# One chunk's half of a Strassen pass's second product is moved between the products of the pass before it

## The chip, the cores and the metric

The kernel runs on one core of a Trainium2 chip. The metric is the device time of one execution in microseconds (us), as a median of several runs. Times inside an execution come from the hardware profiler and are counted from the first instruction.

## The reference

A depthwise causal convolution with 7 softmax-normalised taps for each of 8 heads, then a block that normalises each row, multiplies by two matrices with a ReLU between them, and adds the result to the row:

```
# x: (8, 4224, 192) f32, weight: (8, 7)
w = softmax(weight, axis=-1)                      # per head
y[b,s,h,:] = sum_k w[h,k] * x_pad[b, s+k, h, :]   # 24 channels per head
xn = (y - mean(y)) / sqrt(var(y) + 1e-6) * g_ln   # over the 192 channels
out = y + max(xn @ w_ch1, 0) @ w_ch2              # 192 -> 768 -> 192
```

Everything is 32-bit floating point.

## The kernel before

**Groups.** The 33,792 rows are cut into 18 groups of at most 16 rows for each of 128 partitions. The first three are short and use plain matrix products. The other 15 (numbers 3 to 17, 2048 rows each, the last one with a few exceptions) take the first product (192 to 768, "up", `up_mixed`) and the second (768 to 192, "down", `down_fast`) each by seven half-size products instead of eight: a Strassen-Winograd scheme, in which sums of blocks are formed before and after. While TensorE does group g, VectorE convolves the rows of group g+1, ScalarE scales the outputs of group g-1, and GpSimd starts the DMAs.

**The up stage of a group.** `up_mixed` makes two passes over the 768 hidden features, in chunks of 128: the *small pass* (`one`) does one chunk of each half of the features, the *large pass* (`two`) two chunks of each half. Each pass has the same seven products, always in this order: a11·b11, a12·b21, s2·t0, s3·t1, s1·b12, a22·t2, s4·b22 (in the text "products 1 to 7"; aij are quarters of the group's rows, s1 to s4 sums of these, bij and t0 to t2 quarters of the weights and their sums). `rows_of_tiles` (L523) issues a product: for each of three blocks c of 32 channels, and each chunk i, four matmuls, one for each block q of 32 rows of the TensorE array, which work beside each other. So a product of the small pass has 12 matmuls of 32x128 weights by 256 columns, and one of the large pass 24. The profile counts two records for each matmul.

**The banks.** PSUM has eight banks of 512 f32 for each partition. The up stage splits them into two sets of four, X and Y (L689). Block q writes bank q of the set; chunk i writes columns 256·i to 256·i+255 of it. In the small pass there is one chunk only, so the upper 256 columns of each bank lie unused. The products alternate: in the small pass X, Y, X, Y, X, Y, X; in the large pass Y, X, Y, X, Y, X, Y. One of the two sets is the pass's *chain*: X in the small pass, Y in the large one. Products 1, 3, 5 and 7 add onto each other in it, and each is copied out in between. Product 2 stands alone in the other set, and products 4 and 6 add onto each other there.

**Copying out.** After each product, the set is copied to SBUF by ScalarE (`evict`, L646, the instruction at L660), before the next product that writes this set can start. In the small pass that is 1024 elements for each partition, in two halves of 512 (banks 0 and 1, banks 2 and 3); in the large pass 2048 elements at once. `close` (L662) handles products 2, 5 and 6, which belong onto a sum that is already in SBUF: it copies into a scratch tile and then adds this to the finished product by an accumulating DMA that GpSimd starts (`add_by_dma`, L615), or lets VectorE add directly from PSUM (L666). In the large pass, product 2 is closed chunk by chunk: two copies of 1024 elements to the tile `parts_cs`, and two such DMAs onto `c11` (L724). ScalarE then applies ReLU to `c11` in place (L673), much later, after the copy of product 5.

**Order.** All engines run their instructions in the order written; the schedule is made by hand, and semaphores are placed where one instruction needs what another wrote or frees. The order in the large pass (L709 to L759): product 1 into Y; copy Y to `c11`; product 2 into X; two copies from X to `parts_cs` with the DMAs; a scaling (L938); product 3 into Y; copy Y to `c21`; ReLU; product 4 into X; copy X to `c22`; product 5 into Y; `close`; product 6 into X; VectorE adds X (L666); product 7 into Y; copy with ReLU. The down stage (L859) begins with a bank that product 6 used.

Of the kernel before, what the change touches and what calls it, by code (L numbers as in the profile page):

```python
# [16 lines left out]
def kernel(  # L17
# [45 lines left out]
    NQ = P // C  # L63
# [19 lines left out]
    PAIR = NF // 2 - 1  # L83
    HJ = J // 2
    EARLY = 10
    CH = NC // 2
# [38 lines left out]
    def take_set():  # L125
        i = (turn[0] + 3) // 4 * 4 % 8
        turn[0] = i + 4
        return all_banks[:, i : i + 4]
# [355 lines left out]
    def store_y(g, queue=nc.sync):  # L484
        n = groups[g][2]
        for ps, rows in rows_of_out(g, 0, n):
            queue.dma_start(out=rows, in_=y[g][ps, 0:n].rearrange("p j d -> p (j d)"))
# [32 lines left out]
            return  # L520
        nc.scalar.activation(dst, src, AF.Relu)  # L521

    def rows_of_tiles(banks, left, right, first=True, last=True, split=False, lead=0):  # L523


        chunks, n, t = right.shape[2] // P, left.shape[1], left.shape[3]
        w = n * t

        def one(c, i, q, j1, j2, start):
            rows = slice(C * q, C * q + C)  # L530
            nc.tensor.matmul(  # L531
                banks[:, q, i * w + j1 * t : i * w + j2 * t], right[rows, c, P * i : P * i + P],
                left[rows, j1:j2, c, :], start=start,
                stop=(last and c == left.shape[2] - 1), skip_group_check=split,
            )

        for q in range(NQ // 2 if lead else 0):
            one(0, 0, q, 0, lead, first)
        for c in range(left.shape[2]):
            for i in range(chunks):  # L540
                for q in range(NQ):
                    begun = lead if c == i == 0 and q < NQ // 2 else 0
                    one(c, i, q, begun, n, first and c == 0 and i == 0 and not begun)

    def between(g, f):

# [12 lines left out]
    def up(g):  # L559


        n = groups[g][2]
        hidden_tile(g)
        for f in range(NF):
            banks = take_set()
            rows_of_tiles(banks, yt[g][:, 0:n], w1[:, :, f * P : f * P + P])
            evict_up(g, f, banks[:, :, 0 : n * C])
            if g == 0 and f == 0:
                first_tap(1, heads=(0, H // 2))
            elif g == 0 and f == 1:  # L570
                copies_of_w1(1, [(q, 1) for q in range(NQ)])
                scale_power(words_2[2])
            elif g == 0 and f < 4:
                first_tap(1, heads=(2 * f, 2 * f + 2))
            between(g, f)
# [16 lines left out]
    def quarters_of_y(g):  # L592
        if width(g) == C:
            cuts = [(slice(HJ * h, HJ * h + HJ), slice(0, C)) for h in range(2)]
        else:
            cuts = [(slice(0, J), slice(T * h, T * h + T)) for h in range(2)]
        return [yt[g][:, js, CH * k : CH * k + CH, ts] for js, ts in cuts for k in range(2)]
# [16 lines left out]
    def add_by_dma(dst, src):  # L614
        nc.gpsimd.dma_start(out=dst, in_=src, accum_op=ALU.add)  # L615

    def up_mixed(g, ahead, pending):
# [3 lines left out]
        last = g + 1 == NG  # L621
# [3 lines left out]
        a11, a12, a21, a22 = quarters_of_y(g)  # L625
        s1, s2, s3, s4 = ysums[g]
        done = groups[g - 1][2]

        class Pass:
# [6 lines left out]
                    for h in range(2)  # L636
                ]

            def product(self, to, left, right, first=True, end=True, lead=0):
                rows_of_tiles(to, left, right, first, end, True, lead)  # L640

            def seen(self, banks, f=None):
                src = banks[:, :, 0 : self.n * W] if f is None else banks[:, :, W * f : W * f + W]
# [31 lines left out]
        def parts(pool, tag):  # L675

            room = pool.tile([P, J * D], F32, tag=tag, name=f"parts_{tag}{g}")
            return room.rearrange("p (f q w) -> p f q w", q=NQ, w=W)
# [9 lines left out]

        X, Y = take_set(), take_set()  # L689
        one, two = Pass(PAIR, FC, X, Y), Pass(0, PAIR, Y, X)  # L690
        p = one
        p.product(X, a11, p.b11, True, False, 0 if last else HJ // 2)
        p.evict(X, p.c11)
        p.product(Y, a12, p.b21)
        p.close(p.c11, Y, two.c12[:, 0:1])
        next(pending, None)
        p.product(X, s2, p.t[0], False, False)
        p.evict(X, p.c21)
        p.product(Y, s3, p.t[1], True, False)
        p.evict(Y, p.c22)  # L700
        p.product(X, s1, p.b12, False, False)
        p.close(p.c22, X, two.c12[:, 1:2])
        next(pending, None)
        p.product(Y, a22, p.t[2], False)
        p.close(p.c21, Y, two.c22[:, 0:1])
        p.product(X, s4, p.b22, False)
        p.evict(X, p.c12, True)

        next(ahead)  # L709
        p = two  # L710
        rooms = parts(cpool, "cs"), parts(bpool, "tb")
        p.product(Y, a11, p.b11, True, False)
        p.evict(Y, p.c11)
        p.product(X, a12, p.b21)
        if last:
            (near, near_part), (far, _) = [
                [v[:, :, q : q + 2] for v in (p.c11, rooms[1][:, 0:PAIR])] for q in (0, 2)
            ]
            nc.vector.tensor_tensor(far, far, p.seen(X)[:, :, 2:NQ], op=ALU.add)
            nc.scalar.copy(near_part, p.seen(X)[:, :, 0:2])  # L720
            for f in range(PAIR):
                add_by_dma(*[v[:, f].rearrange("p q w -> p (q w)") for v in (near, near_part)])
        else:
            for f in range(PAIR):  # L724
                p.close(p.c11[:, f : f + 1], X, rooms[0][:, f : f + 1], f)
            if g == 3:
                store_y(g, nc.gpsimd)
        act_scales(0, 1)
        if last:

            for j1 in (0, HJ):
                part, factor = ots[g - 1][:, j1 : j1 + HJ], rstd[g - 1][:, j1 : j1 + HJ]
# [1 line left out]
                    part, part, factor.unsqueeze(2).to_broadcast([P, HJ, D]), op=ALU.mult  # L734
                )
                add_to_out(g - 1, j1, j1 + HJ)
        p.product(Y, s2, p.t[0], False, False)
        p.evict(Y, p.c21)
        one.relu(one.c11)
        p.product(X, s3, p.t[1], True, False)  # L740
# [22 lines left out]
        if last:  # L763

            n = J - fast[g]
# [174 lines left out]
    def add_to_out(g, j1, j2):  # L940
        if groups[g][0] is None:

            j1, j2 = (0, j2) if j2 == groups[g][2] else (0, 0)
        for ps, rows in rows_of_out(g, j1, j2) if j2 else ():
            src = ots[g][ps, j1:j2].rearrange("p j d -> p (j d)")
            step = 4 * D if groups[g][0] is not None else (j2 - j1) * D
            for d0 in range(0, (j2 - j1) * D, step):
                d1 = min(d0 + step, (j2 - j1) * D)
                nc.gpsimd.dma_start(out=rows[:, d0:d1], in_=src[:, d0:d1], accum_op=ALU.add)  # L949
# [66 lines left out]
    for g in range(NG):  # L1016
        mixed, last = g in MIXED, g + 1 == NG
        if g + 2 < NG and g not in (1, 2, 3):
            load_x(g + 2)
        if mixed:  # L1020
            work = up_mixed(g, ahead(g), pending)
            pending = iter(())
        else:
            up(g)
            work = []
        if g == 0:
            early = CH * C // GRP
# [88 lines left out]
```

## Time and profile before

| quantity | value |
|---|---|
| median of 3 runs | 949.95 us (949.79 to 950.6) |
| span of the profiled execution, first to last instruction | 948.1 us |
| TensorE matmul busy | 940.8 us (99%) |
| VectorE / ScalarE / GpSimd busy | 893.7 (94%) / 699.8 (74%) / 342.7 us (36%) |
| granted TensorE clock, mean | 1.000 |
| one typical group (from 447.57 to 502.52 us) | small pass 9.19, large pass 18.43, down 27.33 us |
| copies of 1024 elements from X to `parts_cs` (L660) | 28, mean 1015 ns |
| copies of 2048 elements by ScalarE to `c11`, `c21` and `c22` (L660) | 45, mean 1864 ns |

PE is TensorE's matmul row, PEld its weight loads, DVE VectorE, ACT ScalarE, POOL GpSimd. In the table by stretches each line gives a stretch's bounds and length, then the busy time of each engine with the count of its instructions in brackets, the granted clock, and the DMA share and rate. In a timeline each line gives the start, the time, engine, source line, operation, tiles and count, and in square brackets the idle time before it and what ended it.

### The profile page before, as it was taken

To read this page: it belongs to the slowest core of one execution; us is meant where nothing else is said; L and a number is where in the kernel's file an instruction comes from. 1 tells how busy PE (TensorE), PEld (TensorE's weight loads), DVE (VectorE), ACT (ScalarE), POOL (GpSimd) and SP (SyncE) were. 2 spreads that over 40 slices of the span, in tenths; PEclk is the share of its full clock that TensorE was granted. 3 is DMA by queue.
4 is the path that set the end of the run, shared out by engine and by line. 5 is a ranking of instruction groups with operands and counts; after the bars stand their busy time and mean duration, and the time that the engine had idled before them with its cause. 6 is when DMAs were issued, how large, how long until landed. Compare 5 with 4: busy or idle time off the path is not lost.

```text
span 948.1 us, 38092 instructions
## 1 busy us (share of the span) xinstructions
PE 940.8 (99%) x16910; PEld 751.7 (79%) x16910; DVE 893.7 (94%) x1498; ACT 699.8 (74%) x1250; POOL 342.7 (36%) x478
## 2 busy tenths in 40 slices
PE   8999999999999999999999999999999999999998
PEld 7998896877869687786968898696877869696787
DVE  8999999999999999999999999999999999999867
ACT  6764678596877969687896968779696877867362
POOL 2158422723145141533227141452316341261420
PEclk9999999999999999999999999999999999999999
DMA  8359589689797988979698896969889797778261
GB/s 222 97 151 220 102 235 274 121 190 231 135 270 134 252 162 188 220 132 279 126 252 151 199 221 127 282 131 251 162 194 213 131 274 136 174 137 131 54 114 68
DMA packets 39833, 169.35 MB, mean 179 GB/s; under 512 B 4469, under 2 KB 8182, under 8 KB 33655
## 3 DMA queue, kind: packets, MB, share of 16 engines
q0 software_dynamic: 32992, 107.46, 61.1%
q1 hardware_dynamic: 6672, 59.47, 17.0%
q8 instruction: 132, 2.16, 0.9%
q14 instruction: 31, 0.25, 0.1%
q10 hardware_dynamic: 6, 0.00, 0.0%
HBM read 38.93 MB, written 50.33 MB: 94 GB/s over the span
## 4 chain that ended last, share of the span: by engine, by line
PE 96%; DMA 2%; POOL 1%; ACT 1%; issue 0%; SPq 0%; DVE 0%; ACTq 0%; POOLq 0%
PE ps L531 46%; PE ps L859 44%; PE ps L796 4%; DMA xg<-in_x_dram 1%; DMA room<-room 1%; PE ps L326 1%; ACT room L660 0%; POOL room L615 0%; PE ps L352 0%; POOL d L458 0%; ACT w L360 0%; ACT room L521 0%; POOL r L481 0%; POOL d L476 0%; POOL d L477 0%
## 5 line engine op out<-in xcount | busy, mean ns | idle before, releaser
L415 DVE SCALAR_TENSOR_TENSOR y<-xg,taps,y 128x384 f32<-128x384 f32 (+3 forms) x720 | 364.2, 581 | 2.4 <-DMA y<-room 1.9
L859 PE MATMUL ps<-room,w2sums 128*32 128x256 f32 (+2 forms) x4608 | 245.5, 371 | 0.2 <-issue 0.2
L531 PE MATMUL ps<-yt,w 32*128 32x256 f32 (+2 forms) x4160 | 237.6, 373 | 0.1
L531 PEld LDWEIGHTS ps<-yt,w 32*128 32x128 f32 x4160 | 210.3, 185 | 21.9 <-issue 7.0
L859 PEld LDWEIGHTS ps<-room,w2sums 128*32 128x32 f32 x4608 | 154.7, 110 | 84.9 <-issue 0.8
L660 ACT COPY room<-ps 128x512 f32<-128x512 f32 (+1 forms) x213 | 174.2, 859 | 62.9 <-PE ps L531 62.4
L859 PE MATMUL ps<-room,w 128*32 128x256 f32 (+2 forms) x3456 | 189.2, 371 | 0.0
L826 DVE TENSOR_TENSOR room<-room 128x1024 f32<-128x1024 f32 (+2 forms) x147 | 161.2, 1169 | 21.5 <-PE ps L859 11.1
L859 PEld LDWEIGHTS ps<-room,w 128*32 128x32 f32 x3456 | 113.9, 110 | 67.2 <-DVE room L666 5.0
L531 PE MATMUL ps<-ysums,w1sums 32*128 32x256 f32 x2160 | 127.0, 376 | 0.2 <-issue 0.2
L531 PEld LDWEIGHTS ps<-ysums,w1sums 32*128 32x128 f32 x2160 | 116.2, 185 | 5.4 <-issue 0.6
L949 POOL DMA_DIRECT2D out_dram<-ot x69 | 59.0, 940 | 162.8 <-ACT ot L938 159.2
L865 ACT COPY cs<-ps 128x256 f32<-128x256 f32 (+2 forms) x192 | 70.3, 368 | 45.1 <-PE ps L859 45.0
L407 POOL DMA_DIRECT2D y<-tb x59 | 52.2, 1375 | 137.8 <-ACT room L865 104.6
L673 ACT ACTIVATE room<-room 128x1024 f32<-128x1024 f32 (+1 forms) x89 | 94.4, 1073 | 2.9 <-DMA room<-parts_cs 2.8
L938 ACT ACTIVATE ot<-ot,r 128x192 f32<-128x192 f32 x224 | 94.7, 468 | 0.0
L378 ACT ACTIVATE y<-xg,taps 128x384 f32<-128x384 f32 (+3 forms) x141 | 73.0, 607 | 0.5 <-DMA xg<-in_x_dram 0.5
L446 DVE BATCH_NORM_STATS2 st<-y 128x6 f32<-128x192 f32 x264 | 70.1, 343 | 0.0
L531 PE MATMUL ps<-yt,w1sums 32*128 32x256 f32 x1080 | 68.9, 376 | 0.1
L865 ACT COPY room<-ps 128x256 f32<-128x256 f32 (+2 forms) x96 | 35.4, 370 | 45.0 <-PE ps L859 44.1
L531 PE MATMUL ps<-ysums,w 32*128 32x256 f32 x1080 | 68.3, 374 | 0.0
L396 ACT ACTIVATE tb<-xg,taps 128x384 f32<-128x384 f32 (+1 forms) x120 | 66.1, 628 | 0.0
(120 smaller groups left out, 935.7 us busy)
## 6 DMA issues: line engine op xcount, KB each, us to landing
xg<-in_x_dram SPq DMA_DIRECT2D x14, 2112.0 KB, 16.2
room<-room POOLq DMA_DIRECT2D x45, 512.0 KB, 5.2
out_dram<-ot POOLq DMA_DIRECT2D x59, 384.0 KB, 9.3
y<-tb POOLq DMA_DIRECT2D x58, 384.0 KB, 8.4
out_dram<-y SPq DMA_DIRECT2D x13, 1536.0 KB, 9.4
room<-parts_cs POOLq DMA_DIRECT2D x28, 512.0 KB, 6.9
room<-parts_tb POOLq DMA_DIRECT2D x14, 1024.0 KB, 7.6
xg<-in_x_dram POOLq DMA_DIRECT2D x1, 2112.0 KB, 13.5
```

Of the source, the lines that this page charges most:

```text
L378: nc.scalar.mul(y[g][:, 0:n, cs], xg[g][:, 0:n, cs], taps[:, h, 0:1])
L396: nc.scalar.mul(tb[g][:, 0:n, cs], xg[g][:, 1 : 1 + n, cs], taps[:, h, 1:2])
L415: nc.vector.scalar_tensor_tensor(out=y[g][:, 0:n, cs], in0=t[:, k : k + n, cs], scalar=taps[:, h, k : k + 1], in1=y[g][:, 0:n, cs], op0=AL ...
L446: nc.vector.bn_stats(out=sums[g][:, j, :], in_=y[g][:, j, :])
L531: nc.tensor.matmul(banks[:, q, i * w + j1 * t : i * w + j2 * t], right[rows, c, P * i : P * i + P], left[rows, j1:j2, c, :], start=start, ...
L660: nc.scalar.activation(to, of, AF.Relu) if relu else nc.scalar.copy(to, of)
L673: nc.scalar.activation(c, c, AF.Relu)
L826: nc.vector.tensor_tensor(a[:, *dst, f], a[:, *left, f], a[:, *right, f], op=op)
L859: nc.tensor.matmul(dst[C * q : C * q + C, 0:w], right[:, f, C * c : C * c + C], left[:, f, q], start=(first and f == PAIR), stop=(f == PAI ...
L865: nc.scalar.copy(to[:, c], dst[:, 0:w].rearrange("p (j t) -> p j t", t=t))
L938: nc.scalar.mul(ots[g][:, j, :], ots[g][:, j, :], rstd[g][:, j : j + 1])
L949: nc.gpsimd.dma_start(out=rows[:, d0:d1], in_=src[:, d0:d1], accum_op=ALU.add)
```

## The change

Groups 3 to 16 are changed; the last group keeps its order. The upper 256 columns of the four X banks, which lie unused in the small pass, take chunk 1 of the large pass's product 2 (a12·b21). It is issued in three pieces of four matmuls (one for each channel block c), after products 2, 4 and 6 of the small pass (`early`). In the large pass, product 1 is issued chunk by chunk (all three c of chunk 0, then of chunk 1) in place of channel block by channel block; product 2 has only chunk 0 left (12 matmuls); product 3 goes chunk by chunk too. ScalarE copies the finished chunk 1 of X first (before `c11`), then `c11` in two copies of 1024 elements in place of one of 2048, then chunk 0 of X. The DMA onto chunk 1 of `c11` is started before the one onto chunk 0. `rows_of_tiles` gets a list of (c, i) to go through.

```
+            steps = [(c, i) for c in range(left.shape[2]) for i in range(chunks)]
...
-            one(0, 0, q, 0, lead, first)
-        for c in range(left.shape[2]):
-            for i in range(chunks):
-                for q in range(NQ):
-                    begun = lead if c == i == 0 and q < NQ // 2 else 0
-                    one(c, i, q, begun, n, first and c == 0 and i == 0 and not begun)
+            one(*steps[0], q, 0, lead, first)
+        for s, (c, i) in enumerate(steps):
+            for q in range(NQ):
+                begun = lead if s == 0 and q < NQ // 2 else 0
+                one(c, i, q, begun, n, first and s == 0 and not begun)
...
+        by_chunk = [(c, i) for i in range(PAIR) for c in range(CH)]
+
+        def early(c):
+            if not last:
+                two.product(X, a12, two.b21, False, steps=[(c, PAIR - 1)])
...
         p.product(Y, a12, p.b21)
         p.close(p.c11, Y, two.c12[:, 0:1])
+        early(0)
...
         p.product(Y, s3, p.t[1], True, False)
         p.evict(Y, p.c22)
+        early(1)
...
         p.product(Y, a22, p.t[2], False)
         p.close(p.c21, Y, two.c22[:, 0:1])
+        early(2)
...
         p = two
-        p.product(Y, a11, p.b11, True, False)
-        p.evict(Y, p.c11)
-        p.product(X, a12, p.b21)
...
-            for f in range(PAIR):
-                p.close(p.c11[:, f : f + 1], X, rooms[0][:, f : f + 1], f)
+            c11 = [p.c11[:, f : f + 1] for f in range(PAIR)]
+            part = [rooms[0][:, f : f + 1] for f in range(PAIR)]
+            p.product(Y, a11, p.b11, True, False, steps=by_chunk)
+            p.evict(X, part[PAIR - 1], f=PAIR - 1)
+            for f in range(PAIR):
+                p.evict(Y, c11[f], f=f)
+            p.product(X, a12, p.b21, steps=[(c, i) for c, i in by_chunk if i < PAIR - 1])
+            for f in (PAIR - 1, *range(PAIR - 1)):
+                if f < PAIR - 1:
+                    p.evict(X, part[f], f=f)
+                add_by_dma(c11[f].rearrange(whole), part[f].rearrange(whole))
...
-        p.product(Y, s2, p.t[0], False, False)
+        p.product(Y, s2, p.t[0], False, False, steps=None if last else by_chunk)
```

More of the change, by code (lines that the diff above doesn't have):

```diff
@@ L521, in evict_up, with rows_of_tiles @@
         nc.scalar.activation(dst, src, AF.Relu)
-    def rows_of_tiles(banks, left, right, first=True, last=True, split=False, lead=0):
+    def rows_of_tiles(banks, left, right, first=True, last=True, split=False, lead=0, steps=None):
         chunks, n, t = right.shape[2] // P, left.shape[1], left.shape[3]
         w = n * t
+        if steps is None:
+            steps = [(c, i) for c in range(left.shape[2]) for i in range(chunks)]
         def one(c, i, q, j1, j2, start):
@@ L637, in __init__, with product @@
                 ]
-            def product(self, to, left, right, first=True, end=True, lead=0):
-                rows_of_tiles(to, left, right, first, end, True, lead)
+            def product(self, to, left, right, first=True, end=True, lead=0, steps=None):
+                rows_of_tiles(to, left, right, first, end, True, lead, steps)
             def seen(self, banks, f=None):
@@ L711, in up_mixed @@
         rooms = parts(cpool, "cs"), parts(bpool, "tb")
-        p.product(Y, a11, p.b11, True, False)
-        p.evict(Y, p.c11)
-        p.product(X, a12, p.b21)
         if last:
+            p.product(Y, a11, p.b11, True, False)
+            p.evict(Y, p.c11)
+            p.product(X, a12, p.b21)
             (near, near_part), (far, _) = [
@@ L723, in up_mixed @@
         else:
-            for f in range(PAIR):
-                p.close(p.c11[:, f : f + 1], X, rooms[0][:, f : f + 1], f)
+            whole = "p f q w -> p (f q w)"
+            c11 = [p.c11[:, f : f + 1] for f in range(PAIR)]
+            part = [rooms[0][:, f : f + 1] for f in range(PAIR)]
+            p.product(Y, a11, p.b11, True, False, steps=by_chunk)
+            p.evict(X, part[PAIR - 1], f=PAIR - 1)
+            for f in range(PAIR):
+                p.evict(Y, c11[f], f=f)
[4 more added lines that the diff above has]
+                add_by_dma(c11[f].rearrange(whole), part[f].rearrange(whole))
             if g == 3:
```

## The prediction

> **What bounds the kernel now.** I first read the page's busy shares and its chain of work that ended last.
>
> ```profile
> PE 940.8 (99%) x16910; PEld 751.7 (79%) x16910; DVE 893.7 (94%) x1498; ACT 699.8 (74%) x1250; POOL 342.7 (36%) x478
> ...
> PE 96%; DMA 2%; POOL 1%; ACT 1%; issue 0%; SPq 0%; DVE 0%; ACTq 0%; POOLq 0%
> ```
>
> TensorE bounds the kernel from end to end. The change leaves all its matmuls in, so it can gain only where TensorE now waits, and every new wait counts in full. Since a busy PE need not be a PE at its peak, I cut one typical group (450 us into the span) into its products and asked for the busy table of each stretch.
>
> ```profile
> 447.57:448.98 1.41, 1.41 (x31) 1.37 (x32) 1.41 (x5) 0.37 (x1) 0.74 (x1) 1.00 1.08 209
> 448.98:450.28 1.30, 1.30 (x28) 1.21 (x22) 1.27 (x3) 1.07 (x2) 0.00 (x0) 1.00 1.11 218
> ...
> 455.46:456.76 1.30, 1.30 (x31) 1.22 (x25) 1.30 (x4) 1.03 (x2) 0.00 (x0) 1.00 0.34 60
> 456.76:459.35 2.59, 2.59 (x55) 2.45 (x51) 2.59 (x6) 1.07 (x2) 1.72 (x2) 1.00 0.43 82
> 459.35:461.94 2.59, 2.59 (x55) 2.44 (x51) 2.59 (x6) 1.87 (x1) 0.00 (x0) 1.00 1.09 204
> 461.94:464.53 2.59, 2.59 (x55) 2.45 (x51) 2.59 (x6) 2.18 (x3) 0.86 (x1) 1.00 0.68 128
> ...
> 472.30:475.19 2.89, 2.89 (x55) 2.42 (x47) 2.31 (x2) 1.59 (x2) 0.85 (x1) 1.00 0.68 136
> ```
>
> The first number after the bounds is the length. A small product takes 1.30 us and a large one 2.59, just twice that for twice the matmuls. Small and large pass run at the same rate. So TensorE loses nothing between products 2 of the small and 6 of the large pass: 0.11 us stands at the start (the first matmul is cut in two) and 0.30 at the end (product 7 and the step to the down stage). The waits of PEld inside this group say the same:
>
> ```profile
> PEld ps L531 <- issue: 0.4, 1, 0.4
> PEld ps L859 <- DVE room L666: 0.3, 1, 0.3
> ```
>
> Third, the timeline, for what would hold TensorE if it were faster (start, time, engine, line):
>
> ```profile
> 450.49 1.07 ACT L660 COPY room<-ps 128x512 f32<-128x512 f32 x2 [0.22 <-PE ps L531]
> ...
> 457.17 1.02 ACT L660 ACTIVATE room<-ps 128x1024 f32<-128x1024 f32 x1 [0.37 <-PE ps L531]
> ...
> 459.76 1.87 ACT L660 COPY room<-ps 128x2048 f32<-128x2048 f32 x1 [1.57 <-PE ps L531]
> 461.72 5.36 PEld L531 LDWEIGHTS ps<-ysums,w1sums 32*128 32x128 f32 x96
> ...
> 462.35 1.93 ACT L660 COPY parts_cs<-ps 128x1024 f32<-128x1024 f32 x2 [0.72 <-PE ps L531]
> ...
> 472.78 2.29 DVE L666 TENSOR_TENSOR room<-room,ps 128x2048 f32<-128x2048 f32 x1 [1.06 <-PE ps L531]
> ...
> 475.19 2.75 PEld L859 LDWEIGHTS ps<-room,w 128*32 128x32 f32 x56 [0.33 <-DVE room L666]
> ```
>
> Two things are to be seen. The copy of Y's product 1 ends at 459.76 + 1.87 = 461.63, and product 3, which overwrites Y, loads its first weights at 461.72: it is ready by 0.09 us only, and what covers the copy is product 2, all 24 matmuls of it. And a copy starts 0.21 us after its product in the small pass (450.49 after 450.28) but 0.41 in the large one (459.76 after 459.35, 462.35 after 461.94): the row blocks 2 and 3 lag blocks 0 and 1, since the second half of each small copy comes later, and the lag grows to 0.2 us and stays until the group's end.
>
> **The change, part by part.** Let T be the start of the large pass (456.76 in this group).
>
> *Early pieces.* Each group gets 3 x 4 matmuls more in the small pass: 12 x 1.30/12 = 1.30 us, so T comes 1.30 later. They find no wait to fill there, as the table shows none. Do they add one? The order of the changed program's instructions, with the semaphores that each waits for, shows that each piece waits for ScalarE twice (at row blocks 0 and 2), and that products 3, 5 and 7, which follow, no longer do. So a piece into the upper half of X's banks waits for the copy out of the lower half. It stands where the product behind it stood, one product of the other set after that copy's own, so cover and lag are the same as now: 0. Products 4 and 6 and the large product 1 get 0.43 us more slack, worth nothing. Behind a waiting piece only TensorE's own later matmuls queue.
>
> *Large product 1 and its copies.* In the same order the first copy of `c11` waits for TensorE, and the second follows without a wait of its own: the first one waited for all 24 matmuls, so the order by chunk gives ScalarE no early start. Product 3 has one wait for ScalarE ahead of its 24 matmuls, not one for each chunk: it needs both copies. ScalarE's own queue then: the copy with ReLU (457.17, so T+0.41 to T+1.43), chunk 1 of X (1.01, to T+2.4), then Y. Product 1 ends at T+2.59. The copies start 0.21 to 0.41 later; as the lag at T is about 0.15 (less than now, since product 1 no longer meets a late copy), I take T+2.95. Two copies of 1024 elements take 1.93 as a pair (462.35 row) in place of 1.87: T+4.88. From a copy's end to the next product: at most 0.09 to the load (461.63, 461.72) and 0.22 from load to matmul (461.72, 461.94), but the last step overlaps when TensorE is idle (475.19: load and matmul together). I take 0.15: product 3 starts at **T+5.03**.
>
> *Product 2's cover is halved.* Without a wait, product 3 would start at T+2.59+1.30 = T+3.89. So TensorE stands still for 5.03-3.89 = **1.14 us**. Before, product 3 started at T+5.18. The 1.30 us that left product 2 are thus paid in the small pass and not got back in the large one, but for 0.15. Bounds: with copies starting at +0.41 and 0.31 to the matmul, T+5.24, a net loss of 1.36; with +0.21 and 0.05, T+4.78, a net loss of 0.90.
>
> *After that.* A full stop lines the row blocks up again, so the 0.2 us lag is gone: VectorE's addition of product 6 (472.78) starts 0.2 earlier against the matmuls, and the 0.30 at the stage's end shrinks to about 0.1. Bounds 0 to 0.3; I take 0.2. Nothing else there is late: copies, ReLU and VectorE keep their distances to product 3 or gain.
>
> *DMAs and POOL.* The two DMAs onto `c11` go out after the second copy (about T+4.9) and after chunk 0 of X (about T+5.9, copied behind it on ScalarE), where they were issued at T+6.9 and T+7.8 (L615 at 463.67, two in 1.77 us). ReLU of `c11` reads them at 471.89, T+15.1, or T+14 after the change; they land in 6.9 us in the median. Cost 0. On POOL's queue they pass nothing; SP's queue is untouched.
>
> *The sum.* For each of 14 groups: +1.30 (early) -0.15 (product 3) -0.20 (lag) = +0.95; 14 x 0.95 = 13.3 us. Group 3 has a stall of 0.57 in small product 3 that the profile puts on nothing, taken as unchanged. The profiled span of 948.1 becomes 961.4; the median stands 1.85 above the span, so 949.95 + 13.3 = **963.2 us**.
>
> **A rule weighed.** The order above shows waits between different columns of one bank; the trace of before has no such pair. The Trainium skill, "PSUM — Partial Sum Buffer", section "PSUM bank collisions raise a hardware error", says why: two engines must not touch the same bank and 32-partition quadrant at once, whatever columns they use, and PSUM is to be guarded by bank and not by address. By that rule the sum is the one above; were guarding by address enough, it would be the second rival's. No run here shows the collision itself.
>
> **The rivals.**
>
> *The lag stays.* If the addition of product 6 starts as late as now, the end of the stage gives nothing back: 14 x 1.15 = 16.1, 966. For it: the 0.33 in front of L859 is VectorE's, 2.29 us long. Against it: that row started upon PE, so it moves with PE.
>
> *The copies run by chunk: no loss.* Place: ScalarE's first copy of `c11`. Should it start when chunk 0 is done (T+1.30), it would follow the copy of X at once, T+2.4 to T+3.4, and the second would end at T+4.3. The point from which it decides is whether both are out by T+3.67 and T+4.96, one weight load (0.22) ahead of product 3's chunks at T+3.89 and T+5.18. They would be; product 3 starts on time, the 1.30 comes back, 14 x 0 = 0: 949 to 950. Only the missing second wait in the program's order speaks against it, but plainly.
>
> *A landing becomes the bound.* In even groups POOL's chain (L458 to L481) stands ahead of the small pass's last DMA, which frees `c22` for the copy of large product 4. Once now (at 852.95) that copy waited 0.48 us and TensorE 0.49. The large pass's first part shrinks by 0.15 and that copy comes earlier against T, so it may hit 7 groups: +0.49 x 7 = 3.4, 966.6. Against it: the landing moves 0.43 earlier against T too.
>
> *The change is undone by something else* (VectorE at 94%): VectorE gets about 1 us more time in each group, so no.
>
> **The numbers.** Forecast 0.73 (959.5 to 965.5); lag stays 0.09; landing 0.10; by chunk 0.05; other 0.03, of it 0.02 faster. The bounds per group, 0.90 - 0.30 = 0.60 and 1.36, would give 958.4 and 969.0; both ends need all unknowns at one side, so the range is 959 to 967.5, which leaves about 2 in 10 out. About 0.2% is what a measurement of this kernel can tell from no change. Faster 0.02, same 0.05, slower 0.93.
>
> **What would show it.** Right: PEld with a wait of about 1.1 us for ScalarE's L661 ahead of large product 3 in groups 3 to 16, some 16 us in total; small pass about 10.5 us, large pass about 18.1; the two `c11` copies back to back and starting after product 1's end. Wrong: copies of `c11` starting in the middle of product 1, a large pass near 17.1, or waits inside the small pass.

## The result and the profile after

The changed kernel takes 963.19 us (median of 4 runs, 962.51 to 964.04), the kernel before 950.17 us (4 runs). The ratio is 1.0138, with a 95% interval of 1.0124 to 1.0153: it is slower by 13.0 us. The forecast was 963.2.

The page of the changed kernel, its first part and its chain of work that ended last:

```profile
span 962.2 us, 38078 instructions
...
PE 945.2 (98%) x16910; PEld 751.0 (78%) x16910; DVE 894.1 (93%) x1498; ACT 699.1 (73%) x1264; POOL 341.5 (35%) x478
...
PE 96%; ACT 3%; issue 0%; DMA 0%; DVE 0%; ACTq 0%
```

The work is the same (16910 matmul records, ScalarE as busy as before with 14 instructions more). New is ScalarE with 3% of the chain: TensorE waits for it now. The waits of the weight loads, over the whole span (us in total, times, longest):

```profile
PEld ps L533 <- ACT room L661: 15.9, 14, 1.1
PEld ps L533 <- issue: 6.9, 17, 0.7
...
PEld ps L880 <- DVE room L667: 5.0, 15, 0.3
```

The first line is new: 14 waits for a copy, one in each changed group, 1.1 us each. The other two stood there before with 7.5 and 5.0 us. Here is group 9 of the changed kernel (the group that the prediction was worked out on) by stretches: the small pass, large products 1, 2 and 3, and the last stretch, product 7 with the step to the down stage.

```profile
454.32:464.80 10.48, 10.48 (x200) 10.30 (x200) 10.34 (x21) 6.82 (x13) 2.34 (x3) 1.00 0.70 133
464.80:467.39 2.59, 2.59 (x54) 2.59 (x50) 2.59 (x6) 1.93 (x2) 1.54 (x2) 1.00 0.59 112
467.39:469.73 2.34, 1.61 (x30) 1.21 (x23) 2.34 (x5) 1.98 (x3) 0.00 (x0) 1.00 1.08 201
469.73:472.42 2.69, 2.69 (x48) 2.57 (x52) 2.69 (x6) 1.22 (x2) 1.72 (x2) 1.00 0.96 180
...
480.19:482.89 2.70, 2.70 (x52) 2.25 (x44) 2.29 (x1) 1.43 (x2) 0.68 (x1) 1.00 0.73 143
```

The small pass has grown from 9.19 to 10.48 us, by the three early pieces. Product 2, now with 12 matmuls, fills 2.34 us in place of 1.30: 1.04 of it is a hole, the one stretch where PE is busy for less than its length. Product 3 takes 2.69 in place of 2.59: after the stop its first weight load and its first matmul start together, at 469.73, where before the load ran 0.22 us ahead of the matmul (461.72 and 461.94). The last stretch shrank from 2.89 to 2.70. In all the group's up stage takes 28.57 us in place of 27.61: +0.96. The timeline around the hole:

```profile
465.16 1.02 ACT L661 ACTIVATE room<-ps 128x1024 f32<-128x1024 f32 x1 [0.75 <-PE ps L533]
...
466.08 1.01 ACT L661 COPY parts_cs<-ps 128x1024 f32<-128x1024 f32 x1
467.75 1.93 ACT L661 COPY room<-ps 128x1024 f32<-128x1024 f32 x2 [0.66 <-PE ps L533]
...
469.73 5.06 PEld L533 LDWEIGHTS ps<-ysums,w1sums 32*128 32x128 f32 x96 [1.13 <-ACT room L661]
```

ScalarE has nothing to do for 0.66 us before the first copy of `c11`: it waits for the end of product 1, all of it, although chunk 0 was done 1.3 us earlier. Both copies end at 469.68, and product 3 loads its first weights at 469.73.

The table by product of the two profiled executions adds up: 12 groups by +0.96 (11.5 us), group 3 by +1.08, group 16 by +0.59 (it had a stall of its own before, below), together 13.2 us. The spans differ by 14.1. The opening, before the first changed line, adds 1.4: group 3 starts at 118.19 in place of 116.76 us. The down stages give back 0.5: short stalls in groups 8 and 10 of the profile of before are gone, and group 9 has a smaller one. In the profiles of all kernels here group 3 starts between 116.3 and 118.4, whatever their edits, and such stalls of the down stage come and go too, so neither is put down to the change.

### The profile page after: what moved, and what is told of

Its sections match the earlier page's. It is cut to its first block, busy times and chain, and to the rows that moved or that the text cites. A ratio compares the mean times of both kernels' runs of the same rounds, so it can differ in the third digit from the quotient of the medians.

```text
span 962.2 us, 38078 instructions
## 1 busy us (share of the span) xinstructions
PE 945.2 (98%) x16910; PEld 751.0 (78%) x16910; DVE 894.1 (93%) x1498; ACT 699.1 (73%) x1264; POOL 341.5 (35%) x478
## 3 DMA queue, kind: packets, MB, share of 16 engines
q8 instruction: 132, 2.16, 0.9%
## 4 chain that ended last, share of the span: by engine, by line
PE 96%; ACT 3%; issue 0%; DMA 0%; DVE 0%; ACTq 0%
PE ps L533 46%; PE ps L880 44%; PE ps L817 4%; ACT room L661 3%; PE ps L365 1%; PE ps L326 1%; PE ps L352 0%; ACT room L521 0%; ACT w L360 0%; ACT y L378 0%; PE ps L355 0%; PE ps L335 0%; PE ps L338 0%; DMA room<-in_weight_dram 0%; PE ps L990 0%
## 5 line engine op out<-in xcount | busy, mean ns | idle before, releaser
L533 PE MATMUL ps<-yt,w 32*128 32x256 f32 (+2 forms) x4160 | 240.5, 374 | 0.3 <-ACT room L521 0.3
L661 ACT COPY room<-ps 128x512 f32<-128x512 f32 (+2 forms) x227 | 175.0, 816 | 81.8 <-PE ps L533 81.8
L533 PEld LDWEIGHTS ps<-yt,w 32*128 32x128 f32 x4160 | 214.6, 185 | 18.1 <-issue 6.2
L880 PEld LDWEIGHTS ps<-room,w2sums 128*32 128x32 f32 x4608 | 149.9, 110 | 89.3 <-issue 0.3
L880 PEld LDWEIGHTS ps<-room,w 128*32 128x32 f32 x3456 | 111.3, 110 | 69.7 <-DVE room L667 5.0
L533 PEld LDWEIGHTS ps<-ysums,w1sums 32*128 32x128 f32 x2160 | 113.0, 185 | 20.2 <-ACT room L661 15.9
L616 POOL DMA_DIRECT2D room<-room x45 | 39.4, 874 | 76.1 <-ACT room L661 71.6
L533 PE MATMUL ps<-ysums,w 32*128 32x256 f32 x1080 | 65.5, 374 | 0.0
```

The costliest lines, as they stand in the source:

```text
L533: nc.tensor.matmul(banks[:, q, i * w + j1 * t : i * w + j2 * t], right[rows, c, P * i : P * i + P], left[rows, j1:j2, c, :], start=start, ...
L661: nc.scalar.activation(to, of, AF.Relu) if relu else nc.scalar.copy(to, of)
L880: nc.tensor.matmul(dst[C * q : C * q + C, 0:w], right[:, f, C * c : C * c + C], left[:, f, q], start=(first and f == PAIR), stop=(f == PAI ...
```

## The experiments

The theory, "cover": large product 3 waits until the copies of `c11` have left Y's banks, product 2 is what covers them, and the loss is the cover that was taken out of product 2. The rivals: "pieces", the early pieces cost something in the small pass; "order", going by chunk or copying in two costs something; "copies by chunk", chunk 0 is copied or overwritten ahead of chunk 1, so that the order by chunk brings a gain. Ratios are to the kernel before, run beside each.

### No early pieces, the rest of the change kept

```
-        early(0)
...
-        early(1)
...
-        early(2)
...
-            p.evict(X, part[PAIR - 1], f=PAIR - 1)
...
-            p.product(X, a12, p.b21, steps=[(c, i) for c, i in by_chunk if i < PAIR - 1])
+            p.product(X, a12, p.b21, steps=by_chunk)
...
-                if f < PAIR - 1:
-                    p.evict(X, part[f], f=f)
+                p.evict(X, part[f], f=f)
```

> The changed kernel without its early pieces: product 2 of the large pass is whole again (24 matmuls, by chunk); the order by chunk, the two copies of c11 and the order of the DMAs stay. Theory (cover): large product 3 waits for the copies of Y, and what is lost is the cover that left product 2. Here product 2 covers again: the copies end at T+3.00+1.93 = T+4.93, product 3 loads at T+4.96, no wait, so 950.2 us (949.5 to 951), 13 us below the changed kernel. Rival (order): going by chunk, or copying c11 in two, costs by itself; then it stays clearly above 952. Rival (pieces): the early pieces cost by themselves, each a third; then also 950.2, so this run tells only order from the other two.

Measured: 950.24 us, ratio 1.000 (0.999 to 1.0009). Large products 1 to 3 of group 9 in this run:

```profile
456.95:459.54 2.59, 2.59 (x54) 2.45 (x50) 2.59 (x6) 1.07 (x2) 1.72 (x2) 1.00 0.42 81
459.54:462.13 2.59, 2.59 (x54) 2.45 (x50) 2.59 (x6) 1.93 (x2) 0.00 (x0) 1.00 1.09 204
462.13:464.72 2.59, 2.59 (x54) 2.45 (x50) 2.59 (x6) 2.17 (x3) 0.86 (x1) 1.00 0.68 128
```

Three times 2.59, no hole, while the two copies take the same 1.93 us as in the changed kernel. So the order by chunk and the split copies cost nothing: "order" falls.

### The early pieces alone

```
-            p.product(Y, a11, p.b11, True, False, steps=by_chunk)
+            p.product(Y, a11, p.b11, True, False)
...
-            for f in range(PAIR):
-                p.evict(Y, c11[f], f=f)
+            p.evict(Y, p.c11)
...
-        p.product(Y, s2, p.t[0], False, False, steps=None if last else by_chunk)
+        p.product(Y, s2, p.t[0], False, False)
```

> The changed kernel with products 1 and 3 of the large pass by channel block, and c11 copied in one instruction of 2048 elements, as before; the early pieces and the short product 2 stay. Theory (cover, guarded by bank): the order by chunk does nothing, since both copies of c11 wait for all of product 1 and product 3 for both; one copy takes 1.87 in place of 1.93: 963.2 - 14 x 0.06 = 962.4 us (961.5 to 963.5). Rival (copies by chunk): the order by chunk gives ScalarE an early start or lets product 3 start after one copy; without it the time gets worse by up to 0.9 per group, 975.

Measured: 962.96 us, ratio 1.0132 (1.0118 to 1.0146). Product 2 of group 9 takes 2.28 in place of 2.34 us:

```profile
467.02:469.30 2.28, 1.61 (x30) 1.21 (x22) 2.28 (x6) 1.91 (x2) 0.00 (x0) 1.00 1.02 190
```

Without the order by chunk the hole is even 0.06 shorter, by the one copy in place of two. So the order by chunk does nothing for what it was written for, and "copies by chunk" falls. Why is read from the program's order: ScalarE's first copy waits for all 24 matmuls, product 3 for both copies. In this program the waits go by bank, and both chunks lie in the same banks. A kernel whose waits went by columns was not tried: it would need one engine in a bank while another writes to it.

### Eight useless matmuls in the hole

```
             p.product(X, a12, p.b21, steps=[(c, i) for c, i in by_chunk if i < PAIR - 1])
+            p.product(X, a12, p.b21, False, steps=[(0, PAIR - 1), (1, PAIR - 1)])
```

> The changed kernel with 8 matmuls more in each of the 14 groups, of no use (two channel blocks of chunk 1 of product 2 again, into the upper half of X, that has been copied out), between large product 2 and product 3. TensorE does 8 x 0.108 = 0.86 us more work per group, 12.1 us in all. Theory (cover): they lie wholly in the hole (T+3.89 to T+4.75, and product 3 starts at T+5.03): no change, 963.2 us (962.5 to 965). Rival (pieces, or any loss inside the small pass): no hole stands there, and the work adds: 975.3 us.

Measured: 963.43 us, ratio 1.0135 (1.012 to 1.015): 12.1 us more of matmuls, and no time that these runs can tell. Product 2, the eight matmuls, and product 3 of group 9:

```profile
466.41:467.71 1.30, 1.30 (x31) 1.30 (x27) 1.30 (x3) 0.94 (x2) 0.00 (x0) 1.00 0.98 176
467.71:468.76 1.05, 1.05 (x24) 0.78 (x16) 1.05 (x3) 0.99 (x2) 0.00 (x0) 1.00 1.17 222
468.76:471.45 2.69, 2.69 (x51) 2.56 (x53) 2.69 (x6) 1.37 (x2) 1.72 (x2) 1.00 0.95 181
```

1.30 + 1.05 = 2.35 is product 2's stretch of the changed kernel, now filled but for 0.19 (eight matmuls take 0.86 of the 1.05). The loss is a hole at this place, and nowhere in the small pass.

### One copy of `c11` left out

```
-            for f in range(PAIR):
-                p.evict(Y, c11[f], f=f)
+            p.evict(Y, c11[0], f=0)
```

> The changed kernel without the second copy of c11 (chunk 1 of large product 1 is not copied out, so chunk 1 of c11 is left without it). TensorE's work is as in the changed kernel. Theory (cover): the one copy runs from T+2.95 to T+3.96, product 3 starts at about T+4.11 in place of T+5.03, 0.22 behind product 2; per group +1.30 -1.07 -0.20 = +0.03: 950.6 us (949.5 to 953). Rival (pieces): the loss lies in the small pass and stays: 963. Rival (copies by chunk): product 3's first chunk would wait only for the first copy anyway, and nothing changes.

Measured: 955.1 us, ratio 1.0041 (1.0025 to 1.0057). It went the right way, 8 us below the changed kernel, but it is 4.5 above what was expected, and outside the range. In 12 of the 14 groups of the profile the expectation holds (product 2 at 1.43, the large pass 17.18 in place of 18.09 us). In groups 4 and 14 a new stall stands in product 5. Group 4, products 2 and 5, and the timeline of what product 6 waited for:

```profile
187.06:188.49 1.43, 1.43 (x31) 1.21 (x24) 1.43 (x4) 1.01 (x1) 1.19 (x4) 1.00 0.06 9
...
193.77:198.02 4.25, 2.77 (x52) 2.25 (x44) 4.13 (x8) 2.39 (x3) 0.00 (x0) 1.00 1.08 207
```

```profile
189.20 0.89 POOL L616 DMA_DIRECT2D room<-room  x1
...
196.10 1.86 ACT L661 COPY room<-ps 128x2048 f32<-128x2048 f32 x1 [1.86 <-DMA room<-room]
...
198.02 2.47 PEld L533 LDWEIGHTS ps<-yt,w1sums 32*128 32x128 f32 x48 [1.89 <-ACT room L661]
```

The copy of product 4 to `c22` waits 1.86 us for a DMA that was started at 189.20 and landed at 196.00. That is the small pass's last DMA, onto `c21`, whose source is scratch in `c22`. In even groups GpSimd's chain for the next norm stands ahead of it. Fifteen of its sixteen parts had landed after 4.65 us, the last after 6.81. With one copy left out, the copy to `c22` is due 9.68 us after the large pass's start, 0.91 earlier than in the changed kernel (10.59), so a landing that comes late holds it sooner. This one, at 11.54, would have held the changed kernel too; the one of group 14, at 10.52, would not. That is a reading of one profile, so it was tried:

### The same, with GpSimd's chain behind that DMA

```
         p.close(p.c22, X, two.c12[:, 1:2])
-        next(pending, None)
         p.product(Y, a22, p.t[2], False)
         p.close(p.c21, Y, two.c22[:, 0:1])
+        next(pending, None)
         early(2)
```

> The kernel with one copy of c11 left out (as in the run before it, so chunk 1 of c11 lacks product 1), and in even groups GpSimd's second part of its chain (L458 to L481) behind the DMA onto c21 in place of ahead of it. That DMA is then issued at about T+1.3 in even groups too, in place of T+4.7. Theory: what the run with one copy lost against its expectation (955.1 for 950.6) is the landing of that DMA, for which the copy of large product 4 waits in some even groups; it goes: 951.1 us (950.3 to 952.5). Rival: the loss is in something that TensorE's earlier product 3 meets in all groups: 955.

Measured: 949.9 us, ratio 0.9993 (0.9984 to 1.0003), 1.2 below the expectation's middle and 0.4 below its range. In group 4 the DMA onto `c21` is now issued at 184.39 and has landed at 191.47, 2.7 us before the copy of product 4 starts at 194.15. Product 5 of group 4:

```profile
193.78:196.37 2.59, 2.59 (x53) 2.46 (x49) 2.59 (x6) 2.58 (x3) 0.00 (x0) 1.00 1.01 193
```

2.59 in every group, 27.66 us for each up stage from group 4 to 16. So the stalls in product 5 were that landing: 2.5 of the 4.0 us between the spans of the two profiles. Another 1.3 lay in the down stages of groups 6, 8, 10 and 12 (27.50 to 27.95 us), which take 27.33 here. There the ReLU of `c11` had come 2.0 to 2.4 us late, because it waited for the DMAs onto `c11`, which GpSimd's chain holds back as well. And with one copy left out, the whole loss of the change is gone: the two copies of `c11` against the shortened product 2 are its cause.

### One early piece in place of three

```
-        early(1)
...
-        early(2)
...
-            p.evict(X, part[PAIR - 1], f=PAIR - 1)
...
-            p.product(X, a12, p.b21, steps=[(c, i) for c, i in by_chunk if i < PAIR - 1])
+            p.product(X, a12, p.b21, steps=[s for s in by_chunk if s != (0, PAIR - 1)])
...
-                if f < PAIR - 1:
-                    p.evict(X, part[f], f=f)
+                p.evict(X, part[f], f=f)
```

> The changed kernel with one early piece (channel block 0, behind small product 2); the other two channel blocks of chunk 1 are back in large product 2, which has 20 matmuls. The first matmul of product 2 resets the bank, so the early piece's share is lost from the sum: chunk 1 of product 2 lacks channel block 0. Theory (cover): product 3 starts at T+5.03 as in the changed kernel, with a wait of 0.28 us behind product 2's end at T+4.75. Per group +0.43 for the piece, -0.15 for product 3, -0.20 for the lag that the stop removes: +0.08, in all +1.1: 951.3 us (950 to 953). Rival (pieces): each piece costs a third of the 13 us: 954.5 us.

Measured: 953.06 us, ratio 1.0023 (1.0012 to 1.0035), just outside the range, between the theory's 951.3 and 954.5 for a third. Product 2 (20 matmuls) and product 3 of group 9:

```profile
461.94:464.33 2.39, 2.39 (x47) 2.03 (x39) 2.39 (x6) 1.93 (x2) 0.00 (x0) 1.00 1.06 195
464.33:467.03 2.70, 2.70 (x52) 2.57 (x53) 2.70 (x7) 2.28 (x3) 1.16 (x2) 1.00 0.77 146
```

20 matmuls take 2.16, so the hole is 0.23 and the start after it 0.10: 0.33, for 0.28 expected. Per group that is 27.76 for 27.61 us, +0.15 where +0.08 was expected, and 14 x 0.15 = 2.1 us. By time alone this run would not tell cover from pieces; by the trace it does, since the small pass grew by just the piece's 0.43 and no wait stands in it.

### Product 1's half moved early, in place of product 2's

```
...
+        if not last:
+            two.product(Y, a11, two.b11, False, steps=[(c, PAIR - 1) for c in range(CH)])
         p.product(Y, a22, p.t[2], False)
...
+        chunk_0 = None if last else [(c, 0) for c in range(CH)]
-        p.product(Y, a11, p.b11, True, False)
+        p.product(Y, a11, p.b11, True, False, steps=chunk_0)
         p.evict(Y, p.c11)
         p.product(X, a12, p.b21)
```

> The kernel before, with chunk 1 of large product 1 (12 matmuls into the unused upper half of Y) moved in front of small product 6, in place of product 2's half; product 2 stays whole. Large product 1's first matmul resets the bank, so in chunk 1 product 3 does not add onto product 1: that share is left out of the sums. As many matmuls are moved as by the change. Theory (cover): product 3 needs the copy of Y, which now can start at T+1.66 and end at T+3.53, while product 2 covers 2.59 us; only product 2 itself meets a short wait for the copy of small product 7 (start T+1.53 in place of T+1.30). Product 3 starts at T+4.12 in place of T+5.18: +1.30 -1.06 -0.20 = +0.04 per group: 950.8 us (949 to 953.5). Rival (moving 12 matmuls into the small pass costs by itself): 963.

Measured: 951.43 us, ratio 1.0014 (1.0005 to 1.0023). Product 1's rest, products 2 and 3 of group 9:

```profile
459.04:460.53 1.49, 1.49 (x30) 1.21 (x22) 1.49 (x4) 1.07 (x2) 0.47 (x1) 1.00 0.90 173
460.53:463.22 2.69, 2.69 (x50) 2.57 (x52) 2.69 (x6) 1.87 (x1) 0.39 (x1) 1.00 1.00 187
463.22:465.81 2.59, 2.59 (x52) 2.46 (x48) 2.59 (x6) 2.28 (x3) 0.97 (x2) 1.00 0.62 115
```

Just as many matmuls moved into the small pass, but a loss of 1.4 us and not 13. Only product 2 meets a short wait (0.19, and 0.10 for the start), for the copy of small product 7. Product 3 meets none, because product 2 covers its copy. Moving matmuls is cheap; moving them out from under a copy is not.

### VectorE's addition in two halves

```
-                    nc.vector.tensor_tensor(c, c, self.seen(banks), op=ALU.add)
+                    for qs in (slice(0, 2), slice(2, NQ)):
+                        half = c[:, :, qs]
+                        nc.vector.tensor_tensor(half, half, self.seen(banks)[:, :, qs], op=ALU.add)
```

In the kernel before:

> The kernel before, with VectorE's addition of product 6 (L666, 2048 elements, 2.29 us) in two halves of two banks each, in all passes that use it. The down stage begins with one bank, so it waits for one half. Theory: TensorE's 0.30 us at the end of the up stage are 0.21 of lag of row blocks 2 and 3 and 0.09 of VectorE: 0.09 x 15 = 1.4 us less, 948.8 us (948.2 to 949.8). Rival: the 0.30 is all VectorE's (the 0.33 in front of the down stage): 0.30 x 15 = 4.5 us less, 945.7. Rival: the second half, or the longer sum of two instructions, holds the down stage's second block or VectorE's own chain: 950 or more.

Measured: 950.07 us, ratio 0.9997 (0.9988 to 1.0006). No gain: neither the theory's 1.4 us nor the 4.5 of the first rival. The end of group 9's up stage, by stretch and by timeline:

```profile
473.21:476.10 2.89, 2.89 (x54) 2.43 (x46) 2.51 (x3) 1.60 (x2) 0.85 (x1) 1.00 0.67 136
```

```profile
473.50 2.35 DVE L668 TENSOR_TENSOR room<-room,ps 128x1024 f32<-128x1024 f32 x2 [0.30 <-PE ps L531]
475.94 1.23 DVE L837 SCALAR_TENSOR_TENSOR room<-room 128x1024 f32<-128x1024 f32 x1
476.10 1.01 PEld L861 LDWEIGHTS ps<-room,w 128*32 128x32 f32 x22 [0.33 <-DVE room L668]
```

The first half was out at about 474.7, 1.4 us before the load at 476.10, and both were out at 475.85, 0.25 before it (in the kernel before 0.12: 472.78 + 2.29 = 475.07, load at 475.19). VectorE was done sooner and the load came no sooner, so no late second half holds it either. Still the profile names VectorE for the 0.33: the name is only that of the event that came last before the load. In the changed kernel:

> The changed kernel with VectorE's addition of product 6 in two halves of two banks. The end of the up stage is 2.70 us there for product 7 in place of 2.59. Theory (switch): the 0.11 is the step from row blocks to the down stage's column blocks, no matter what VectorE does, as in the run that split the addition in the kernel before: no change, 963.2 us (962.4 to 964), and 2.70 stays. Rival (VectorE): it goes to 2.59: 0.11 x 15 = 1.6 us less, 961.6.

Measured: 963.25 us, ratio 1.0137 (1.0122 to 1.0153). The last stretch is as long as without the split:

```profile
478.85:481.55 2.70, 2.70 (x52) 2.25 (x44) 2.35 (x2) 1.43 (x2) 0.69 (x1) 1.00 0.72 143
```

In both runs with the split VectorE is done 2.63 us after product 7's start; the load comes at 2.89 in one and at 2.70 in the other. So VectorE holds neither kernel's end. In every group whose TensorE stops in the large pass for 0.13 us or more the last stretch is 2.70, in every kernel here, and in those without a stop 2.89. That holds inside the kernel before too: its group 16 has a hole of 0.45 in product 5, then product 6 takes 2.69 and the last stretch 2.70.

## Why the prediction was right, and where its reasons were not

| step | predicted | measured in group 9 |
|---|---|---|
| early pieces, small pass longer by | 1.30 | 10.48 - 9.19 = 1.29, no wait in it |
| first copy of `c11` starts | T+2.95 | 467.75 - 464.80 = T+2.95 |
| both copies are out | T+4.88 | T+4.88 |
| product 3 starts | T+5.03 | records at T+4.93, 0.10 lost at the start: T+5.03 |
| TensorE stands still | 1.14 | 1.04 + 0.10 = 1.14 |
| gain at the stage's end | 0.20 | 2.89 - 2.70 = 0.19 |
| net, per group | +0.95 | +0.96 |

- **What bounds.** TensorE had no wait to give back; that was read from products of 1.30 and 2.59 us, and the eight useless matmuls confirm that only a hole is free. The 0.11 at the group's start was put down to the first matmul's being cut in two. Group 17, where it is not cut, loses 0.10 there too (product 1 takes 1.40), so that reason fails; the sum does not use it.
- **The wait of product 3** came at the place, of the length and for the reason that was named. That both copies wait for all of product 1, and product 3 for both, was in the program's order; the early pieces alone show that the order by chunk does nothing. The prediction said that the trace of before has no wait between different columns of one bank. It has one: the copy of chunk 0 alone to `parts_cs` starts at 462.35, 0.41 after all of product 2 (461.94), just as the copies of whole sets do, though the last four matmuls of product 2 (0.43 us) are all of chunk 1. The Trainium skill, "PSUM — Partial Sum Buffer", section "PSUM bank collisions raise a hardware error", says to guard by bank and quadrant; these waits agree with that, and what would happen without them no run shows.
- **The gain at the end: the number held, the reason only in half.** The prediction let the stop undo the lag of row blocks 2 and 3, VectorE's addition of product 6 start earlier for it, and the end shrink with that. Splitting that addition changes nothing in either kernel, so VectorE never held the end, and that step fails. The lag itself is right, and TensorE's own matmul records show it. In product 7 of the kernel before, the matmuls of blocks 2 and 3 start 0.20 us behind those of blocks 0 and 1, and in the changed kernel 0.01. In both the down stage's first matmul starts 0.30 after the last one of product 7. So the down stage waits for TensorE's own late blocks, and 0.19 goes with the lag; 0.11 stays in any case. One group of the run with the split addition lies in between: group 14 had a stop of only 0.04 in product 5, a lag of 0.06 was left, and its last stretch took 2.75.
- **The rivals.** *The lag stays*: no, 2.70. *Copies by chunk*: no. *A landing becomes the bound*: not in the changed kernel, whose product 5 takes 2.59 us in all groups of the profile, though by little: in group 14 the DMA landed at T+10.60, and the copy that needs it was due at T+10.59. The mechanism is real, and was met where one copy was left out and product 3 came earlier: 0.75 and 1.77 us in two even groups.
- **Groups 3 and 16** were priced like the others; they gave +1.08 and +0.59, 0.25 less than two typical groups. Group 16 had a stall of 0.45 in product 5 before, by the same landing, and lost it in the changed kernel.
- **Luck.** The forecast of 963.2 and the median of 963.19 agree better than the method can: runs of one kernel differ by 1.5 us and more, the kernel before came out at 950.17 in place of 949.95, and groups 3 and 16 were off by 0.12 and 0.37 in opposite directions.
- **What stays open.** The run with one early piece lost 2.7 us by the clock and some 2 in the up stages of its trace, and the one with a copy left out 4.7 by the clock and some 3 in the up stages of its trace; a single profile does not show how often late landings occur in the other runs (those with a copy left out lie between 952.71 and 955.22).

## What to carry to other kernels

When matmuls are moved away from where TensorE is busy anyway, ask what they were covering: here 12 matmuls of product 2 hid the copy out of the other set of banks, and TensorE stood still for 1.14 us where they had stood. Before splitting a copy or a product "so that the next one can start earlier", read in the program's order whether the waits follow: chunks in the same bank were waited for together, so neither the copy nor the product behind it started earlier. And before mending a wait, test the engine that the profile names for it: at the stage's end it named VectorE in both kernels, and what counted was TensorE's own last row blocks.

## What the runs showed of the hardware

- A stop of TensorE costs its wait and 0.10 us more: the product behind every stop takes 2.69 or 2.70 in place of 2.59 us, after holes of 0.13 us (one copy left out) to 1.66 (its group 4), the changed kernel's 1.04 among them.
- The step from the up stage (32x128 tiles of the array) to the down stage (128x32 tiles) takes 0.11 us that no wait for another engine explains, 2.70 for 2.59 after a stop. The Trainium skill, "TensorEngine Tiling (Array Packing)", section "Key Properties", states that changing the tiling mode drains TensorE; the 0.11 agrees with that, without proving it.
- Row blocks of TensorE that wait for separate copies run out of step, and stay so until TensorE stops. By the matmul records of group 9 of the kernel before, blocks 2 and 3 start 0.01 us behind blocks 0 and 1 in small product 2. From product 3 on, the first whose blocks wait for two half copies, they start 0.15 behind, and from product 7 to the end of the large pass 0.20. That costs nothing between the products, which follow each other every 1.30 or 2.59 us, and 0.19 us where the stage ends.
- An accumulating DMA of 512 KB in SBUF (`room<-room`) has landed with fifteen of its sixteen parts after 4.5 to 5 us in most cases, but the last part can come up to 2.2 us later (4.51, then 6.68 us, in one case of the run with one copy). A schedule that relies on the median meets this tail in some groups.
